# A gated linear recurrence followed by a gated feed-forward layer on one core: a new order of the first part, channel loads in two pieces of 48 rows, and two state copies on another engine

## The chip, the cores and the metric

The kernel runs on one core of a Trainium2 chip. Its engines work side by side, each through its own instructions in program order, and wait for one another by semaphores: TensorE (PE, with its weight loads PEld), VectorE (DVE), ScalarE (ACT), GpSimd (POOL), and SyncE (SP), which here only issues DMA transfers. The metric is the device time of one execution in microseconds (us), median of several runs. Lower is better.

## The reference

Cut to what matters: a recurrence over 768 steps for 4 batches and 8 heads of size 48, whose result goes through a feed-forward layer with a sigmoid gate.

```
for t in range(S):
    cur = einsum('bhd,bhe->bhde', u * k[t], v[t])
    y[t] = einsum('bhd,bhde->bhe', r[t], state + cur)
    state = w * state + einsum('bhd,bhe->bhde', k[t], v[t])
x = y.transpose(0, 2, 1, 3).reshape(3072, 384)
out = (sigmoid(x @ w_gate) * (x @ w_val)) @ w_out      # 384 -> 1536 -> 384
```

## The kernel before

The recurrence is done in 12 chunks of 64 steps. A chunk has two groups of heads (g = 1 first, then g = 0), so there are 24 groups n = 0 to 23; even n are g = 1. For a group, TensorE makes scores between the chunk's steps, applies them and the state to the values, and adds the chunk's own products to the state. The results of two chunks fill a tile of 512 columns, x, for the feed-forward layer, which runs over 12 blocks f of 128 hidden units. All 32-bit products there are split into a high and a low part, three matmuls for one. The weights come as 64-bit words and are turned into those two parts on the chip (once, in the first part of the program).

The first part (groups 0 to 7, all weights, and the feed-forward work of the first tile) is written out by hand: the text `START` is a list of steps, each a letter and a number, and every engine gets its instructions in the order of this list. After it, a loop carries the other five tiles. The steps that this document names:

- `L.n`, `X.n`, `W.f`: SP issues the load of a group's channels (`load_channels`, r and k with channels on partitions: 128 rows of 4 KB, of which rows 48 to 63 and 112 to 127 are padding), of its tokens (k and v with steps on partitions), of a block of weights.
- `A.n` (ACT), `R.n` (POOL) or `Rv.n` (DVE), `k.n` (DVE, in place): scale the channels; `T.n` (POOL) or `Tv.n` (DVE): scale the tokens.
- `Z.n` (PE): scores, 64 matmuls into the one tile `sc`; `K.n` (DVE): copy them through masks (L355). `I.n` (PE): from state and scores to y, two banks of PSUM; `O.n` (PE): the chunk's products, into the same two banks. `h.n` (ACT), `l.n` (DVE): high and low part of y into the tile x; `F.n`: six or fewer small transfers from SBUF to SBUF that move 16 rows of x to their places (fills). `d.n` (ACT) decays the state, `s.n` (DVE) adds the products to it, or for the first chunk (n = 0, 1) copies them, L428.
- `c.f` (ACT), `j.f` (DVE, three operations), `w.f` (ACT), `o.f` (POOL) or `ov.f` (DVE): unpack a block of weights; `c0`, `j0`, `w0`, `o0`, `o0v` do halves of block 0.
- `U.i` (PE, L495): the up products of work item i, two banks of PSUM; `g.i` (ACT), `m.i` (DVE), `H.i` (ACT), `q.i` (POOL) or `qv.i` (DVE): the gate and its two parts; `D.i` (PE, L533): the down products. Items 0 and 1 are blocks 0 and 1 for the first chunk's 256 columns, 2 and 3 the same for the second, and item i from 4 is block i - 2 for all 512.
- `tk`, `ti`, `tp` (DVE), `tt` (PE), `tn` (ACT): tables of powers of w. `tc` (POOL, ACT): constants.

Tiles come from pools: channels had three buffers in turn, tokens three, and the PSUM pool `ring`, which holds the banks of `I` and `U`, has three banks. A step that takes a bank waits until the last reader of what was in it is done.

Of the kernel before, what the change touches and what calls it, by code (L numbers as in the profile page):

```python
# [9 lines left out]
F32 = mybir.dt.float32  # L10
# [28 lines left out]


START = """
L.0 tc A.0 tk ti.1 tp W.0 X.0 k.0 Rv.0 c0.0 ti.0 c0.1 L.1 j0.1 A.1 Z.0 K.0 tt L.2 k.1 I.0 Rv.2 A.2
R.1 X.1 tn h.0 T.0 X.3 Z.1 k.2 T.1 l.0 L.3 K.1 O.0 s.0 j0.0 W.1 A.3 I.1 w0.1 o0v.1 h.1 l.1 L.4 R.3
w0.0 c.1 X.2 F.0 Z.2 K.2 W.2 o0.0 O.1 s.1 j.1 Tv.3 X.6 U.0 g.0 c.2 m.0 I.2 k.3 w.1 W.4 W.7 ov.1 d.2
T.2 O.2 h.2 l.2 X.4 s.2 H.0 Z.3 K.3 A.4 q.0 k.4 R.4 c.4 j.2 U.1 g.1 I.3 O.3 L.7 L.5 m.1 d.3 h.3 H.1
l.3 A.5 D.0 w.2 R.5 Z.4 T.4 s.3 K.4 F.2 U.2 k.5 g.2 m.2 q.1 D.1 H.2 U.3 g.3 Z.5 j.4 m.3 X.5 I.4 O.4
W.3 L.6 T.5 H.3 d.4 R.6 X.7 ov.2 h.4 q.3 q.2 c.3 K.5 W.5 s.4 w.4 l.4 U.4 j.3 D.2 g.4 m.4 A.6 H.4 D.3
ov.4 qv.4 w.3 I.5 O.5 d.5 W.6 h.5 c.5 D.4 k.6 ov.3 l.5 c.6 s.5 U.5 A.7 g.5 j.5 w.5 U.6 g.6 j.6 w.6
ov.5 c.7 Z.6 m.5 m.6 K.6 U.7 H.5 qv.5 W.9 g.7 j.7 H.6 D.5 qv.6 o.6 I.6 Tv.6 w.7 W.8 k.7 d.6 D.6 O.6
m.7 Rv.7 H.7 s.6 h.6 c.8 l.6 ov.7 U.8 g.8 q.7 F.6 j.8 c.9 j.9 D.7 w.8 U.9 g.9 ov.8 Z.7 W.11 m.9 w.9  # L50
U.10 H.9 m.8 W.10 H.8 qv.8 D.8 g.10 o.9 K.7 q.9 D.9 m.10 I.7 c.11 j.11 c.10 H.10 qv.10 D.10 h.7 T.7
d.7 j.10 w.10 O.7 l.7 s.7 U.11 w.11 ov.10 g.11 ov.11 U.12 m.11 H.11 F.7 g.12 m.12 q.11 H.12 q.12 D.11
U.13 g.13 D.12 m.13 H.13 q.13
"""


# [1 line left out]
def rwkv_then_moe(ctx: ExitStack, tc: tile.TileContext, wd, ch, tk, rt, ut, wt, rk0, vn0, wd0, out):  # L58
    nc = tc.nc
# [7 lines left out]
    ring = ctx.enter_context(tc.tile_pool(name="ring", bufs=3, space=PSUM))  # L67
    pacc = ctx.enter_context(tc.tile_pool(name="pacc", bufs=1, space=PSUM))
    main = ctx.enter_context(ExitStack())
    ach = main.enter_context(tc.tile_pool(name="ach", bufs=3))  # L70
    atk = main.enter_context(tc.tile_pool(name="atk", bufs=3))
    adk = main.enter_context(tc.tile_pool(name="adk", bufs=2))
    xp = main.enter_context(tc.tile_pool(name="xp", bufs=2))
# [332 lines left out]
    def states(n):  # L406
        g = GROUPS[n][1]
        st = state[0:112, 8 * g * D : 8 * (g + 1) * D]
        return g, st.rearrange("q (p s x) -> q p s x", p=2, s=2)
# [129 lines left out]
    def accumulators():  # L539
        return [pacc.tile([P, 512], F32, name=f"acc{d}") for d in range(3)]  # L540
# [77 lines left out]
    for step in START.split():  # L618
        name, _, arg = step.partition(".")
# [68 lines left out]
    with tc.If(bad != 0):  # L688
        with ExitStack() as g:
# [3 lines left out]
            st = gp.tile([P, NP, B, D], F32, name="st")  # L693
# [18 lines left out]
            with tc.For_i(0, NC) as c:  # L712
                for p in range(NP):
                    nc.sync.dma_start(
                        out=rkc[:, p].rearrange("q a b i -> q (a b i)"),
                        in_=rk0[bass.ds(c, 1), p].rearrange("o q x -> (o q) x"),
                    )
                with tc.For_i(0, C) as i:
                    for lo, side in ((0, 1), (64, 0)):
# [18 lines left out]
                    for lo in (0, 64):  # L738
                        y = one_bank()
# [11 lines left out]
                    out=xg[bass.ds(c, 1)].rearrange("o q p t -> (o q) p t"),  # L751
                    in_=yc.rearrange("q p b i -> q p (b i)"),
# [3 lines left out]
            with tc.For_i(0, NC, 2) as c:  # L756
                for j in range(3):
                    for to, lo, n, p in (
# [3 lines left out]
                            out=xr[to : to + n, j],  # L762
                            in_=xg[bass.ds(c, 2), lo : lo + n, p].rearrange("c q t -> q c t"),
# [4 lines left out]
                m = Moe(x, accumulators(), slice(0, 512))  # L768
# [103 lines left out]
```

## Time and profile before

| what | value |
|---|---|
| median of 3 runs | 541.75 us (540.87 to 541.93) |
| the profiled execution's own time | 540.73 us |
| its span in the trace | 538.9 us |
| busy in the span: PE / PEld / DVE | 518.4 / 425.6 / 216.4 us |
| busy in the span: ACT / POOL | 171.3 / 174.8 us |
| chain that ended last: PE, DMA, DVE | 91%, 4%, 1% of the span |
| HBM read, written | 40.12 MB, 4.72 MB |

The span is what the trace covers; the profiled execution's own time is 1.8 us longer, and the median of the runs shown is 1.0 us above that. A busy time of PE counts pipelined matmuls from start to modelled end, so PE can read as busy while it works below its pace. Times in the trace are counted from the start of the span.

### The profile page before, as it was taken

What the parts mean: (1) busy time and instruction counts of PE and PEld (TensorE: products, weight loads), DVE (VectorE), ACT (ScalarE), POOL (GpSimd) and SP (SyncE); (2) the same over time, 40 slices, a digit from 0 to 9 for tenths busy, and PEclk for the clock granted to TensorE, in tenths of its full rate; (3) what the DMA queues carried; (4) which work ended last, traced back from release to release, by engine and by line L of the source; (5) the groups of instructions that cost most, each with busy time, mean ns of one, the idle gap of its engine ahead of it and who ended that gap; (6) DMA issues with size and microseconds to landing.
All of it is one profiled execution on the core that took longest, in us unless ns stands there. A gap on an engine that the chain in (4) does not pass through costs nothing.

```text
span 538.9 us, 12058 instructions
## 1 busy us (share of the span) xinstructions
PE 518.4 (96%) x5268; PEld 425.6 (79%) x5268; DVE 216.4 (40%) x375; ACT 171.3 (32%) x354; POOL 174.8 (32%) x159
## 2 busy tenths in 40 slices
PE   2889999999999999999999999999999999999996
PEld 2778878788788887888888888888888887888885
DVE  7999989912343342432413414313414311111111
ACT  5485755522132322231332222312322212221121
POOL 3424022122814444244145144143242311111120
PEclk9999999999999999999999999999999999999998
DMA  8895705053022214220303402203400001100001
GB/s 318 312 338 217 286 1 186 15 205 128 2 86 86 66 50 144 85 74 12 95 3 103 145 5 82 65 30 106 144 1 16 11 2 19 60 1 1 0 1 63
DMA packets 15706, 48.03 MB, mean 89 GB/s; under 512 B 2368, under 2 KB 5056, under 8 KB 14240
## 3 DMA queue, kind: packets, MB, share of 16 engines
q1 hardware_dynamic: 15360, 46.81, 25.4%
q8 instruction: 43, 0.70, 0.5%
q10 hardware_dynamic: 288, 0.39, 0.2%
q14 instruction: 15, 0.12, 0.1%
HBM read 40.12 MB, written 4.72 MB: 83 GB/s over the span
## 4 chain that ended last, share of the span: by engine, by line
PE 91%; DMA 4%; DVE 1%; SPq 1%; issue 1%; ACT 0%; POOL 0%; DVEq 0%; ACTq 0%; POOLq 0%
PE ring L495 56%; PE acc L533 27%; PE ring L313 5%; PE sc L341 2%; DMA xt<-xt 1%; DMA chan<-in_ch 1%; PE sc L396 1%; DMA wr<-in_wt 1%; SPq L457 1%; PE sc L533 1%; POOL dec L294 0%; DVE wf L236 0%; DVE wx L246 0%; ACT wx L243 0%; ACT wf L229 0%
## 5 line engine op out<-in xcount | busy, mean ns | idle before, releaser
L495 PE MATMUL ring<-xt,wx 128*128 128x512 f32 (+1 forms) x1332 | 316.4, 391 | 1.4 <-DMA xt<-xt 1.2
L495 PEld LDWEIGHTS ring<-xt,wx 128*128 128x128 f32 x1332 | 246.1, 190 | 56.6 <-issue 1.3
L517 POOL TENSOR_TENSOR h<-sg,h 128x512 fp32r<-128x512 f32 (+1 forms) x68 | 86.7, 1276 | 298.8 <-ACT h L513 298.8
L533 PE MATMUL acc<-h,wx 128*128 128x512 f32 (+1 forms) x666 | 161.1, 383 | 0.0
L508 DVE TENSOR_TENSOR sg<-ring,sg 128x512 f32<-128x512 f32 (+1 forms) x74 | 49.9, 676 | 275.6 <-PE ring L495 275.6
L533 PEld LDWEIGHTS acc<-h,wx 128*128 128x128 f32 x666 | 119.6, 188 | 24.4
L504 ACT ACTIVATE sg<-ring 128x512 f32<-128x512 f32 (+1 forms) x74 | 43.4, 587 | 184.3 <-PE ring L495 181.2
L513 ACT CAST h<-sg 128x512 fp32r<-128x512 f32 (+1 forms) x74 | 45.3, 613 | 112.0 <-DVE sg L508 111.1
L415 ACT ACTIVATE state<-state,every 112x96 f32<-112x96 f32 x80 | 23.5, 365 | 26.2 <-PE ring L313 26.2
L294 POOL TENSOR_TENSOR dec<-chan,every 128x512 f32<-128x512 f32 x21 | 25.9, 1233 | 17.0 <-DMA chan<-in_ch 12.7
L453 DVE TENSOR_TENSOR xt<-ring,xt 112x256 fp32r<-112x256 f32 (+1 forms) x52 | 20.0, 419 | 24.9 <-ACT xt L449 24.4
L341 PE MATMUL sc<-dec,chan 48*64 48x64 f32 x768 | 17.4, 231 | 7.9 <-DVE dec L294 7.9
L355 DVE COPY_PREDICATED score<-masks,sc 128x512 f32<-128x512 int32 x32 | 23.9, 745 | 1.5 <-PE sc L341 0.6
L449 ACT CAST xt<-ring 112x256 fp32r<-112x256 f32 (+1 forms) x52 | 17.1, 373 | 19.6 <-PE ring L313 17.0
L341 PEld LDWEIGHTS sc<-dec,chan 48*64 48x64 f32 x768 | 15.0, 145 | 9.3 <-DVE dec L294 7.9
L313 PE MATMUL ring<-score,toks 64*48 64x64 f32 (+1 forms) x768 | 18.7, 230 | 3.7 <-POOL dec L294 1.6
L304 POOL TENSOR_TENSOR toks<-toks,tabn 128x384 f32<-128x384 f32 x20 | 21.1, 1059 | 1.7 <-ACT tabn L194 1.6
L313 PEld LDWEIGHTS ring<-score,toks 64*48 64x48 f32 (+1 forms) x768 | 15.3, 133 | 5.1 <-POOL dec L294 1.8
L313 PEld LDWEIGHTS ring<-dec,state 48*48 48x48 f32 (+1 forms) x704 | 12.4, 127 | 8.3 <-issue 7.4
L300 DVE TENSOR_TENSOR chan<-chan,every 128x512 f32<-128x512 f32 x24 | 17.2, 715 | 0.9 <-ACT dec L273 0.9
L246 POOL TENSOR_TENSOR wx<-wf,wx 128x1152 fp32r<-128x1152 f32 (+1 forms) x3 | 6.8, 2262 | 31.9 <-ACT wx L243 31.9
L282 POOL TENSOR_TENSOR dec<-dec,toks 128x384 f32<-128x384 f32 x16 | 16.3, 1017 | 1.2
(61 smaller groups left out, 260.0 us busy)
## 6 DMA issues: line engine op xcount, KB each, us to landing
wr<-in_wt SPq DMA_DIRECT2D x11, 1152.0 KB, 8.0
chan<-in_ch SPq DMA_DIRECT2D x24, 512.0 KB, 4.9
toks<-in_tk SPq DMA_DIRECT2D x24, 400.0 KB, 5.0
out_y<-wf SPq DMA_DIRECT2D x16, 256.0 KB, 2.3
dec<-in_rt SPq DMA_DIRECT2D x16, 192.0 KB, 2.6
xt<-xt SPq DMA_DIRECT2D x30, 64.0 KB, 2.3
wr<-in_wt SPq DMA_DIRECT2D x2, 576.0 KB, 5.4
xt<-xt SPq DMA_DIRECT2D x12, 32.0 KB, 5.1
```

Source lines behind the costliest of these rows:

```text
L294: eng.tensor_tensor(v4(t[:, 0]), v4(chan[n][:, 0]), bc2(table_of(n)), ALU.mult)
L304: eng.tensor_tensor(v4(k), v4(k), bc2(tabn[:, 4 * g : 4 * g + 4]), ALU.mult)
L313: nc.tensor.matmul(yb[n][bank][64 * half : 64 * half + m, cs], lhsT, rhs, start=first, stop=stop, skip_group_check=True,)
L341: nc.tensor.matmul(sc[64 * gm : 64 * gm + 64, be ^ gm, o : o + C], kk[row, cs : cs + C], rr[row, cs : cs + C], start=True, stop=True,)
L355: nc.vector.copy_predicated(t.rearrange("q (b m i) -> q b m i", b=2, m=4), masks[:, m].bitcast(I32).unsqueeze(1).unsqueeze(1).broadcast_to ...
L415: nc.scalar.activation(st[:, p, s], st[:, p, s], AF.Copy, scale=pw[0:112, 4 * g + 2 * p + s, 64:65],)
L495: nc.tensor.matmul(o[:, self.cols], w[a][:, g * DM + kt * P : g * DM + (kt + 1) * P], self.x[:, kt, b, self.cols], start=(k == 0), stop=(k ...
L504: nc.scalar.activation(sg[:, c], self.pair[f][0][:, c], AF.Sigmoid)
L508: nc.vector.tensor_tensor(sg[:, c], self.pair.pop(f)[1][:, c], sg[:, c], ALU.mult)
L513: nc.scalar.copy(out=h[:, 0, c], in_=sg[:, c])
L517: eng.tensor_tensor(h[:, 1, c], self.sg.pop(f)[:, c], h[:, 0, c], ALU.subtract)
L533: nc.tensor.matmul(acc[:, to], w[a][:, 2 * DM + d * P : 2 * DM + (d + 1) * P], h[:, b, cols], start=(f == 0 and k == 0 and self.cols.start ...
```

## The change

Three things are changed. First, `START` is a new list: the same work in another order, with one `o0`, one `T` and one `q` going from POOL to DVE (as `o0v`, `Tv`, `qv`) and one `ov` going from DVE to POOL (as `o`). Second, the channels have three named buffers that are passed on by hand (a buffer is free again after its group's scores); the first three loads are whole, and each later one is two transfers of 48 rows, which leave out the padding. Third, a step `sa` does the state copy of groups 0 and 1 with `nc.scalar.copy` (ACT) in place of `nc.vector.tensor_copy` (DVE).

```diff
-L.0 tc A.0 tk ti.1 tp W.0 X.0 k.0 Rv.0 c0.0 ti.0 c0.1 L.1 j0.1 A.1 Z.0 K.0 tt L.2 k.1 I.0 Rv.2 A.2
...
+tk ti.1 L.0 tc A.0 L.1 tp tt Rv.0 k.0 A.1 W.0 X.0 L.3 Z.0 c0.0 ti.0 k.1 R.1 K.0 I.0 c0.1 j0.0 j0.1
+X.1 Z.1 h.0 l.0 tn T.0 K.1 w0.0 L.2 A.2 O.0 o0v.0 X.2 W.1 w0.1 k.2 T.2 Rv.2 Tv.1 sa.0 I.1 o0v.1 A.3
+L.4 h.1 Z.2 l.1 O.1 c.1 k.3 j.1 Rv.3 F.0 W.2 sa.1 X.3 X.5 U.0 W.4 T.3 g.0 w.1 K.2 I.2 c.2 h.2 ov.1
...
-    ach = main.enter_context(tc.tile_pool(name="ach", bufs=3))
+    ach = main.enter_context(tc.tile_pool(name="ach", bufs=1))
...
+    CHANNELS = slice(0, D), slice(64, 64 + D)
     chan, toks = {}, {}
+    cbuf = [ach.tile([P, 2, 512], F32, name=f"chan{i}") for i in range(3)]
 
     def load_channels(n):
         c, g = GROUPS[n]
-        chan[n] = ach.tile([P, 2, 512], F32, name="chan")
-        nc.sync.dma_start(out=chan[n], in_=ch[c, g])
+        whole = len(chan) < 3
+        chan[n] = cbuf.pop(0)
+        for rows in (slice(0, P),) if whole else CHANNELS:
+            nc.sync.dma_start(out=chan[n][rows], in_=ch[c, g, rows])
...
+        cbuf.append(chan[n])
...
-    def add_state(n):
+    def add_state(n, copy=nc.vector.tensor_copy):
...
-                nc.vector.tensor_copy(st[:, :, s], y)
+                copy(out=st[:, :, s], in_=y)
```

Where instructions now stand. On DVE, at the start of the program (after the tables in `every`), the rows were the keys of group 0 (L300), its queries (L294), a reciprocal, half a block of weights (L235 to L237), and the first masked copy (L355):

```order
L156 TENSOR_TENSOR every<-every 128x8x32 x2
L300 TENSOR_TENSOR chan<-chan,every 128x512
L294 TENSOR_TENSOR dec<-chan,every 128x512
L172 RECIPROCAL every<-every 128x4x32
L235 TENSOR_SCALAR wf<-wf 128x576
L236 SCALAR_TENSOR_TENSOR wf<-wr,wf 128x576
L237 SCALAR_TENSOR_TENSOR wf<-wr,wf 128x576
L355 COPY_PREDICATED score_101<-masks,sc 128x512 x2
```

In the changed kernel (its lines are 4 or 5 higher) they are:

```order
L160 TENSOR_TENSOR every<-every 128x8x32 x2
L298 TENSOR_TENSOR dec<-chan_95,every 128x512
L304 TENSOR_TENSOR chan_95<-chan_95,every 128x512
L176 RECIPROCAL every<-every 128x4x32
L304 TENSOR_TENSOR chan_96<-chan_96,every 128x512
L360 COPY_PREDICATED score_104<-masks,sc 128x512 x2
L239 TENSOR_SCALAR wf<-wf 128x576
```

The queries now stand ahead of the keys, the keys of group 1 ahead of the first masked copy, and the weights behind it.

On PE, in the second half of the first part, the scores of group 7 (L341, `Z.7`) stood alone between two up products (L495, `U.9` and `U.10`):

```order
L495 MATMUL ring<-xt,wx 128x512 x18
L341 MATMUL sc<-dec,chan 64x64 x16
L341 MATMUL sc<-chan,dec 64x64 x16
L495 MATMUL ring<-xt,wx 128x512 x18
L533 MATMUL acc_428<-h,wx 128x512
```

Now they stand (L345) right behind the products of group 6 (L317, `O.6`), which themselves follow `I.6`, and ahead of a down product (L538, `D.6`):

```order
L317 MATMUL ring<-toks 64x48 x2
L317 MATMUL ring<-toks 48x48 x2
L345 MATMUL sc<-dec,chan_97 64x64 x16
L345 MATMUL sc<-chan_97,dec 64x64 x16
L538 MATMUL acc_427<-h,wx 128x512
```

Three separate groups of small matmuls, `I.6`, `O.6` and `Z.7`, have become one.

On SP, the rows ahead of the first fills (L457) were:

```order
L100 DMA chan<-in_ch 128x1024 x2
L105 DMA toks<-in_tk 128x800 x2
L100 DMA chan<-in_ch 128x1024
L223 DMA wr<-in_wt 128x1152
L100 DMA chan<-in_ch 128x1024
L105 DMA toks<-in_tk 128x800
L457 DMA xt<-xt 16x2x256 x6
```

And now:

```order
+L104 DMA chan_97<-in_ch 128x1024
+L109 DMA toks<-in_tk 128x800
+L104 DMA chan_95<-in_ch 48x1024 x2
+L109 DMA toks<-in_tk 128x800
+L227 DMA wr<-in_wt 128x1152
+L104 DMA chan_96<-in_ch 48x1024 x2
+L462 DMA xt<-xt 16x2x256 x6
```

One token load went behind the fills, and two channel loads ahead of them (`L.2` and `L.4`) are pairs of 48 rows.

## Rows read from the trace of the kernel before

**Rows 1.** Windows: busy us of each engine in stretches, with counts; granted clock; DMA.

```profile
core 0: us, PE busy (x) PEld busy (x) DVE busy (x) ACT busy (x) POOL busy (x), PEclk, DMA share, GB/s
20.00:40.00 20.00, 16.18 (x403) 14.62 (x403) 19.55 (x34) 13.24 (x32) 5.47 (x6) 1.00 0.88 315
40.00:60.00 20.00, 19.27 (x347) 17.08 (x346) 19.79 (x28) 12.74 (x28) 6.33 (x7) 1.00 0.72 269
60.00:80.00 20.00, 19.82 (x231) 15.61 (x231) 17.64 (x22) 11.54 (x19) 3.98 (x2) 1.00 0.18 74
104.00:160.00 56.00, 56.00 (x398) 45.31 (x391) 17.83 (x31) 15.14 (x27) 19.38 (x16) 1.00 0.32 104
```

**Rows 2.** Timeline of DVE, start: start us, duration, line, [idle before <-releaser].

```profile
6.54 0.69 DVE L300 TENSOR_TENSOR chan<-chan,every 128x512 f32<-128x512 f32 x1 [0.93 <-ACT dec L273]
7.15 0.68 DVE L294 TENSOR_TENSOR dec<-chan,every 128x512 f32<-128x512 f32 x1
7.76 0.94 DVE L172 RECIPROCAL every<-every 128x128 f32<-128x128 f32 x1
...
15.32 1.49 DVE L355 COPY_PREDICATED score<-masks,sc 128x512 f32<-128x512 int32 x2 [0.60 <-PE sc L341]
```

**Rows 3.** Timeline of DVE, 16 to 56 us.

```profile
16.71 0.60 DVE L428 COPY state<-ring 112x192 f32<-112x192 f32 x2
...
19.55 0.75 DVE L246 TENSOR_TENSOR wx<-wf,wx 128x576 fp32r<-128x576 f32 x1
...
27.37 0.55 DVE L304 TENSOR_TENSOR toks<-toks,tabn 128x384 f32<-128x384 f32 x1
...
36.96 0.42 DVE L508 TENSOR_TENSOR sg<-ring,sg 128x256 f32<-128x256 f32 x1
37.29 1.72 DVE L453 TENSOR_TENSOR xt<-ring,xt 48x256 fp32r<-48x256 f32 x4
...
41.02 1.25 DVE L300 TENSOR_TENSOR chan<-chan,every 128x512 f32<-128x512 f32 x1
...
50.66 0.75 DVE L235 TENSOR_SCALAR wf<-wf 128x1152 int32<-128x1152 int32 x1
...
54.12 0.68 DVE L508 TENSOR_TENSOR sg<-ring,sg 128x512 f32<-128x512 f32 x1
```

**Rows 4.** Timeline of PE matmuls, 7 to 42 us.

```profile
8.80 1.08 PE L341 MATMUL sc<-chan,dec 48*64 48x64 f32 x32
...
23.02 4.21 PE L495 MATMUL ring<-xt,wx 128*128 128x256 f32 x18
...
35.13 0.57 PE L313 MATMUL ring<-toks 64*64 64x48 f32 x29
...
39.24 2.53 PE L495 MATMUL ring<-xt,wx 128*128 128x256 f32 x18 [1.18 <-DMA xt<-xt]
```

**Rows 5.** Timeline of PE weight loads, 46 to 105 us: starts of groups of small matmuls.

```profile
46.95 0.17 PEld L313 LDWEIGHTS ring<-dec,state 48*64 48x64 f32 x5 [0.57 <-issue]
...
58.90 8.31 PEld L495 LDWEIGHTS ring<-xt,wx 128*128 128x128 f32 x36
67.58 0.56 PEld L341 LDWEIGHTS sc<-dec,chan 48*64 48x64 f32 x32 [0.37 <-issue]
...
78.84 0.55 PEld L313 LDWEIGHTS ring<-toks 64*64 64x64 f32 x32 [0.35 <-issue]
...
103.50 0.54 PEld L313 LDWEIGHTS ring<-toks 64*64 64x64 f32 x32 [0.35 <-issue]
104.09 0.99 PEld L495 LDWEIGHTS ring<-xt,wx 128*128 128x128 f32 x5
```

**Rows 6.** Timeline of ACT: the nearest copy from PSUM.

```profile
12.87 0.51 ACT L194 COPY tabn<-acc 128x192 f32<-128x192 f32 x2
```

**Rows 7.** DMA, 3 to 12 us (whole loads only): packets; q1's share of 16 engines.

```profile
DMA packets 1004, 3.55 MB, mean 395 GB/s; under 512 B 106, under 2 KB 106, under 8 KB 1004
q1 hardware_dynamic: 1004, 3.55, 98.5%
```

**Rows 8.** DMA, 105.1 to 107.5 us (fills of 16 rows only).

```profile
DMA packets 57, 0.13 MB, mean 55 GB/s; under 512 B 25, under 2 KB 25, under 8 KB 57
q1 hardware_dynamic: 57, 0.13, 34.0%
```

More of the change, by code (lines that the diff above doesn't have):

```diff
@@ L41 @@
 START = """
-L.0 tc A.0 tk ti.1 tp W.0 X.0 k.0 Rv.0 c0.0 ti.0 c0.1 L.1 j0.1 A.1 Z.0 K.0 tt L.2 k.1 I.0 Rv.2 A.2
[L43 to L53, printed above, removed]
+tk ti.1 L.0 tc A.0 L.1 tp tt Rv.0 k.0 A.1 W.0 X.0 L.3 Z.0 c0.0 ti.0 k.1 R.1 K.0 I.0 c0.1 j0.0 j0.1
+X.1 Z.1 h.0 l.0 tn T.0 K.1 w0.0 L.2 A.2 O.0 o0v.0 X.2 W.1 w0.1 k.2 T.2 Rv.2 Tv.1 sa.0 I.1 o0v.1 A.3
+L.4 h.1 Z.2 l.1 O.1 c.1 k.3 j.1 Rv.3 F.0 W.2 sa.1 X.3 X.5 U.0 W.4 T.3 g.0 w.1 K.2 I.2 c.2 h.2 ov.1
+m.0 Z.3 L.5 L.7 H.0 W.3 l.2 R.4 O.2 q.0 K.3 d.2 s.2 j.2 U.1 g.1 I.3 D.0 T.5 A.4 k.4 h.3 l.3 w.2 d.3
+Z.4 F.2 o.2 O.3 m.1 X.4 H.1 X.7 s.3 R.5 U.2 A.5 L.6 qv.1 W.11 g.2 m.2 U.3 c.3 D.1 K.4 H.2 qv.2 k.5
+c.4 D.2 Tv.4 g.3 I.4 m.3 d.4 O.4 j.3 H.3 s.4 h.4 l.4 Z.5 K.5 A.7 q.3 w.3 ov.3 U.4 g.4 m.4 D.3 I.5 O.5
+d.5 j.4 R.7 H.4 W.5 s.5 X.6 h.5 l.5 W.6 W.7 w.4 q.4 ov.4 c.5 U.5 W.10 g.5 m.5 A.6 Tv.6 R.6 H.5 c.6
+D.4 j.5 U.6 qv.5 D.5 W.8 W.9 k.6 w.5 g.6 k.7 Z.6 m.6 ov.5 c.7 H.6 j.6 U.7 g.7 K.6 I.6 O.6 q.6 d.6 h.6
+m.7 H.7 Z.7 w.6 j.7 qv.7 T.7 D.6 ov.6 w.7 s.6 D.7 K.7 c.8 l.6 U.8 o.7 g.8 j.8 U.9 w.8 m.8 g.9 ov.8
+m.9 H.8 q.8 U.10 c.9 D.8 H.9 q.9 j.9 g.10 c.10 m.10 j.10 w.9 F.6 I.7 d.7 O.7 H.10 w.10 qv.10 D.9 D.10
+ov.9 s.7 c.11 o.10 h.7 l.7 F.7 U.11 g.11 j.11 m.11 H.11 q.11 w.11 U.12 g.12 ov.11 m.12 H.12 D.11 U.13
+g.13 m.13 H.13 q.12 D.12 qv.13
 """
@@ L600, in rwkv_then_moe @@
         "k": keys, "T": token_keys, "Z": scores, "K": keep, "I": apply, "O": outer,
-        "d": decay_state, "s": add_state, "h": x_high, "l": x_low, "F": fills, "D": finish,
+        "d": decay_state, "s": add_state, "sa": lambda n: add_state(n, nc.scalar.copy), "h": x_high, "l": x_low, "F": fills, "D": finish,
         "tc": constants, "tk": channel_table, "ti": inverses, "tp": token_powers,
```

## The prediction

> **What bounds the kernel now.** I read the stretches first. From 104 us on PE is busy for the whole of each stretch, and the change leaves that part as it is [rows 1]. Ahead of it PE falls short: of 20 us it is busy 16.18 in 20 to 40 us, then 19.27 and 19.82. In 20 to 60 us it is DVE that never rests (19.55 and 19.79 of 20), and the DMA share is high in the same place (0.88, 0.72) [rows 1]. So the start is bound by DVE's chain, with loads close behind, and PE's own pace takes over at about 40 us. The seam is U.2, the first product of the second chunk: its input is the low part l.3, which DVE does from 37.29 for 1.72 us, so until 39.01 [rows 3], and U.2 starts at 39.24, the trace naming the fills as what it waited for [rows 4]. Behind U.2 the matmuls follow each other, but each group of small matmuls that comes after large ones starts with a bubble: 0.37 us at 67.58, 0.35 at 78.84, 0.35 at 103.50 [rows 5]. The end is therefore the time of U.2, plus PE's work behind it, plus the bubbles and waits in it. Both orders have the same matmuls ahead of U.2 and behind it: I.0 to I.3, Z.0 to Z.4, U.0, U.1, D.0 ahead.
>
> **Term 1, the start up to U.2.** DVE's chain runs without a break from 6.54 us to l.3, but for one wait of 0.60 us for Z.1 [rows 2]. What changes in it:
> - The queries of group 0 go ahead of the keys. DVE stood idle 0.93 us before the keys, waiting for ACT [rows 2]; the queries (0.61 us from their start at 7.15 to the next at 7.76) need the load alone and fit in. Gain 0.61.
> - The masked copy K.0 now comes soon after Z.0, which it must wait for. Z.0 needs keys and queries: it can start when the keys end, 6.54 + 0.69 = 7.23, against 7.83 before, so its second half, which ended at 8.80 + 1.08 = 9.88 [rows 4], ends near 9.3. DVE by then has done keys, reciprocal and the keys of group 1: 6.54 + 0.61 + 0.95 + 0.6 = 8.7. A new wait of 0.65; but K.1 no longer waits (two halves of weights stand ahead of it), so the old 0.60 goes. Net cost 0.05.
> - Work ahead of l.3: in come o0v.0 (0.75), Tv.1 (0.55) and the queries of group 3 (0.68); out go both state copies (0.60 each), Tv.3 (0.55) and m.1 (0.42) [rows 2, 3]. Net -0.2.
> - l.3 so ends at 39.01 - 0.61 + 0.05 - 0.2 = 38.25. But O.3, which shares its banks with l.3, now comes after it and ahead of U.2: 0.6 us on PE [rows 4]. U.2 starts at 38.9, not 39.24: **-0.3 us**. The bounds: down to 38.4 if durations are all at their shortest in the new order (the chain holds slower stretches where POOL is at work, 1.25 us for keys that else take 0.69 [rows 2, 3]); up to 39.6 if two more of them fall so.
>
> The state copies on ACT have no row; the nearest are two ACT copies of 128x192 from PSUM, 0.51 us together [rows 6], against 0.60 on DVE [rows 3], and ACT is busy only 13 of 20 us [rows 1]. I take 0.5. They free the banks for I.1 and for U.0's second half; sa.0 can run from O.0's end (near 16.5) and I.1 is ready near 16.9, so the cover is 0 to 0.4 us, and without it I.1 would start up to 0.5 later, hidden as long as l.1 waits for its turn on DVE (near 19.9).
>
> **Loads.** At the whole loads' pace, 9 us x 16 engines x 98.5% for 3.55 MB, a 4 KB row costs an engine 0.164 us [rows 7]. A whole load is 8 rows to an engine, 1.31 us; a pair of 48 rows is 6, so 0.98. The only rows with fewer partitions are the fills, 16 rows: 2.4 us x 16 x 34.0% for 57 - 25 = 32 packets of 4 KB, 0.41 us each [rows 8]. A pair could so cost 2.45. I take the low end, since the packets come from HBM as those of the whole loads do, and keep the other for the range. Ahead of the fills for U.0 this makes: one token load less (400 KB at 395 GB/s, 1.04 us) and two pairs at -0.33 each, so the fills come 1.7 us earlier; at the high end 1.2 later. U.0 itself is ready at about 22.8, when O.1 behind l.1 is done, against 23.02 before [rows 4], so the low end is hidden. The loads ahead of the fills for U.2 leave over 2 us in either case. A second transfer costs SP another issue, which nothing waits for.
>
> [...]
>
> **Term 2, behind U.2.** Groups of small matmuls behind large ones, from U.2 to U.11, before: [Z.5 I.4 O.4], [I.5 O.5], [Z.6], [I.6], [O.6], [Z.7], [I.7], [O.7], eight. After: [I.4 O.4 Z.5], [I.5 O.5], [Z.6], [I.6 O.6 Z.7], [I.7 O.7], five. Three bubbles of 0.35 to 0.37 less [rows 5]: **-1.07 us**. Besides, I.4 waited 0.57 us in its middle for a bank [rows 5]; two down products now stand ahead of it, so this may go too. I count it at nothing, as new waits of that size are likely, and keep it as a bound.
>
> Are there new waits? DVE's list behind U.2 has m.2 ahead of K.4 and m.4 ahead of j.4, so DVE stands idle until U.2 and U.4 end (about 1.7 and 1.0 us). The narrowest place behind is U.5: its second bank is free after l.5, and DVE does j.4 (54.12 - 50.66 = 3.46 [rows 3]), s.5 and half of l.5 between U.4's end and that, 0.25 + 0.62 + 3.46 + 0.53 + 0.4 = 5.3 us. PE meanwhile has D.3 (1.1), I.5 and O.5 with their bubble (2.4) and U.5's first half (a quarter of the 8.31 us of U.5 and U.6 [rows 5], 2.1): 5.6. It holds by 0.3 us. The same count gives 1.1 at U.7 and 0.6 at D.7.
>
> **The sum.** -0.3 - 1.07 = -1.4. The profiled execution took 540.73, so the same one would take 539.3; the median of the runs shown is 541.75, and I forecast **540.4 us**. Less than 0.2% (1.08 us) can't be told from no change here.
>
> **Rivals.**
> - **The new waits take it back.** Place: DVE behind U.2. It idles some 3 to 4 us there that it did not before, and if it comes 1 us late to U.5 or D.7, most of term 2 is gone: -1.4 + 0.3 to 1.1, near 541.3. For it: the margins of 0.3 and 0.6. Against it: at U.7 and U.8 over 1 us.
> - **The pairs are slow.** At 0.41 us a row the fills land 1.2 us later than before and U.0 with them; h.2 and l.2 follow U.0, so U.2 moves too, by about 1.3: 541.65, no change that shows. For it: rows 8. Against it: all else in rows 7 and 8 differs too. [...]
> - **Slower: DVE is late by 3 us.** Where POOL works beside it DVE's keys took 1.25 instead of 0.69 [rows 2, 3]. One block 0 half and one token scaling moved to DVE, but POOL now does o.2 just beside K.4 to m.3. From U.2 to U.7 DVE has 26.8 us of work and about 4 us of waits; if contention adds 3 us, l.5, ov.5 and qv.7 are late and PE waits 2.7 us in sum: 541.75 - 1.4 + 2.7 = 543.0. It costs more than it gains from 1.7 us on. Against it: POOL's share there is as before, and before's DVE rows have their contention in them.
>
> **Chances and range.** Forecast as it stands 0.50; new waits 0.26; slow pairs 0.12; late DVE 0.12. Faster by over 0.2% is the first case, and hardly any of the others; slower by over 0.2% is the last and a rest of the third: 0.50 faster, 0.36 same, 0.14 slower. The low end is the sum of the favourable bounds: U.2 at 38.4 (-0.85), term 2 (-1.07), I.4's wait (-0.57), so -2.5: 539.2. The high end leaves out half of the late DVE: 542.4. The forecast's own case holds 539.2 to 541.1.
>
> **What would show it.** U.2 near 38.9 and preceded by O.3, with no wait for fills; 0.68 us queries beginning near 5.6; five bubbles instead of eight between U.2 and U.11, and U.11 near 102.7 instead of 104.09 [rows 5]; channel pairs landing at about 1.0 us apart when the queue is full. I am wrong if a pair takes near 2 us, if U.5's second half or D.7 waits for DVE, or if U.2 is not earlier although l.3 is.

## The result, and the profile after

The changed kernel is slower: 545.28 us in the median of 6 runs (544.32 to 547.40) against 541.74 for the kernel before (540.87 to 541.99), a ratio of 1.0069 with the interval 1.0047 to 1.0090. The forecast was 540.4 and the range ended at 542.4. The execution that was profiled is the longest of the six (547.40 us, span 545.6), so what it lost is 2 us more than what a middling one loses.

The stretches, in the columns of [rows 1]:

```profile
20.00:40.00 20.00, 17.55 (x482) 15.83 (x479) 18.57 (x30) 13.59 (x33) 5.28 (x5) 1.00 0.88 272
40.00:60.00 20.00, 17.04 (x266) 15.81 (x257) 13.77 (x23) 10.37 (x26) 5.84 (x4) 0.83 0.79 260
60.00:80.00 20.00, 19.57 (x232) 15.61 (x232) 18.85 (x22) 11.96 (x21) 5.66 (x4) 1.00 0.58 243
104.00:160.00 56.00, 55.82 (x438) 45.22 (x430) 22.25 (x35) 17.17 (x32) 20.53 (x16) 1.00 0.32 88
```

Read against [rows 1], only 40 to 60 us stands out: PE is busy 17.04 us instead of 19.27, DVE 13.77 instead of 19.79, and the granted clock is 0.83 where it was 1.00. The DMA share from 20 to 40 us is the same 0.88, but it moves 272 GB/s instead of 315: the queue was as busy and moved less. From 104 to 160 us PE is busy 55.82 us instead of 56.00, so little is lost there. The very end of the program is another matter, and comes last in this section.

The timeline of PE matmuls, with the rows that answer to [rows 4] (U.0, then the last of O.3, then U.2 and U.3 together):

```profile
24.52 3.77 PE L500 MATMUL ring<-xt,wx 128*128 128x256 f32 x18
39.72 0.66 PE L317 MATMUL ring<-toks 64*64 64x48 f32 x30 [0.41 <-DVE xt L458]
43.16 6.73 PE L500 MATMUL ring<-xt,wx 128*128 128x256 f32 x36 [2.78 <-DMA xt<-xt]
```

U.2 starts at 43.16 instead of 39.24, and PE stood idle for 2.78 us waiting for a fill. DVE was ready long before. Its rows, which answer to [rows 2, 3], are the queries of group 0, the keys of group 1, l.3 (done at 39.66) and m.2, which waits for U.2:

```profile
5.57 0.68 DVE L298 TENSOR_TENSOR dec<-chan,every 128x512 f32<-128x512 f32 x1
...
7.96 1.72 DVE L304 TENSOR_TENSOR chan<-chan,every 128x512 f32<-128x512 f32 x1
...
37.92 1.74 DVE L458 TENSOR_TENSOR xt<-ring,xt 48x256 fp32r<-48x256 f32 x4
...
47.44 0.42 DVE L513 TENSOR_TENSOR sg<-ring,sg 128x256 f32<-128x256 f32 x1 [4.88 <-PE ring L500]
```

What held the fills shows in the DMA issues from 30 to 36 us (KB each, and us from issue to landing):

```profile
wr<-in_wt SPq DMA_DIRECT2D x1, 1152.0 KB, 10.2
chan<-in_ch SPq DMA_DIRECT2D x2, 192.0 KB, 7.0
xt<-xt SPq DMA_DIRECT2D x3, 32.0 KB, 9.5
```

The block of weights is W.3, issued at 32.36 and landed at 42.58; the fills for U.2 stand right behind it and landed from 42.80 to 43.87. W.3 itself stands behind the pairs of L.5 and L.7, and L.7 could only be issued at 31.53, when the scores of group 3 had freed its buffer (the first row is SP's issues of both pairs, the second the end of Z.3 on PE):

```profile
25.55 6.76 SPq L104 DMA_DIRECT2D chan<-in_ch  x4
...
30.80 0.65 PE L345 MATMUL sc<-chan,dec 48*64 48x64 f32 x32
```

The pace of the queue while it held hardly anything but the first pair (12 to 14 us) was half of what whole loads gave in [rows 7], at a full share:

```profile
DMA packets 136, 0.39 MB, mean 197 GB/s; under 512 B 28, under 2 KB 28, under 8 KB 136
q1 hardware_dynamic: 136, 0.39, 101.6%
```

One load of both pieces is 393 KB, 2.0 us at 197 GB/s; a whole one is 524 KB, 1.33 us at the 395 GB/s of [rows 7]. The windows around U.2:

```profile
40.00:42.00 2.00, 0.38 (x26) 0.25 (x16) 1.60 (x4) 2.00 (x8) 2.00 (x1) 0.82 0.87 220
42.00:44.00 2.00, 0.84 (x4) 0.88 (x5) 0.56 (x1) 0.13 (x1) 1.60 (x2) 0.50 0.32 73
44.00:46.00 2.00, 2.00 (x11) 2.00 (x11) 0.00 (x0) 0.49 (x2) 0.00 (x0) 0.50 1.04 318
46.00:48.00 2.00, 2.00 (x12) 2.00 (x11) 0.56 (x2) 1.15 (x2) 0.00 (x0) 0.50 1.00 250
48.00:50.00 2.00, 2.00 (x18) 2.00 (x18) 1.97 (x4) 1.76 (x3) 0.00 (x0) 0.98 0.99 401
```

PE did little from 40 to 43 us, and then ran at the lower clock (0.50 until 48 us) for most of the 36 products of U.2 and U.3, in 6.73 us. A wait on a transfer (2.78 us) has become a wait and a slow stretch behind it.

That is not all that was lost. U.11 starts 4.58 us later than before (108.67 against 104.09 [rows 5]), but the span is 6.7 us longer. Most of the rest stands behind the last computation. These are the last rows of DVE, of the kernel before and of the changed one:

```profile
533.99 0.42 DVE L563 COPY sg<-sc 128x256 f32<-128x256 f32 x1
...
538.98 0.42 DVE L568 COPY sg<-sc 128x256 f32<-128x256 f32 x1
```

From the end of that row to the end of the span, with only the last of the result to move out, it is 4.5 us before (span 538.9) and 6.2 us now (545.6): 1.7 us more.

### The profile page after: what moved, and what is told of

It reads as the page before. It is cut to its first block, busy times and chain, and to the rows that moved or that the text cites. A ratio compares the mean times of both kernels' runs of the same rounds, so it can differ in the third digit from the quotient of the medians.

```text
span 545.6 us, 12119 instructions
## 1 busy us (share of the span) xinstructions
PE 520.5 (95%) x5268; PEld 427.9 (78%) x5268; DVE 218.9 (40%) x373; ACT 171.6 (31%) x358; POOL 179.0 (33%) x157
## 4 chain that ended last, share of the span: by engine, by line
PE 81%; DVE 2%; issue 1%; POOL 1%; ACT 0%; POOLq 0%; DVEq 0%
PE ring L500 49%; PE acc L538 25%; PE ring L317 4%; PE sc L345 2%; PE sc L401 1%; PE sc L538 1%; DVE wf L241 0%; DVE score L360 0%; POOL h L522 0%; DVE wf L240 0%; DVE wx L250 0%; POOL dec L298 0%; POOL dec L286 0%; POOL dec L284 0%; DVE sg L513 0%
## 5 line engine op out<-in xcount | busy, mean ns | idle before, releaser
L522 POOL TENSOR_TENSOR h<-sg,h 128x512 fp32r<-128x512 f32 (+1 forms) x67 | 88.7, 1323 | 311.1 <-ACT h L518 300.7
L538 PE MATMUL acc<-h,wx 128*128 128x512 f32 (+1 forms) x666 | 160.7, 382 | 0.0
L538 PEld LDWEIGHTS acc<-h,wx 128*128 128x128 f32 x666 | 119.7, 188 | 24.4
L317 PE MATMUL ring<-score,toks 64*48 64x64 f32 (+1 forms) x768 | 18.9, 230 | 4.5 <-DVE score L360 3.4
L317 PEld LDWEIGHTS ring<-score,toks 64*48 64x48 f32 (+1 forms) x768 | 15.4, 133 | 5.8 <-issue 3.6
L241 DVE SCALAR_TENSOR_TENSOR wf<-wr,wf 128x1152 int32<-128x1152 int32 (+1 forms) x13 | 19.1, 1473 | 0.4
L345 PE MATMUL sc<-dec,chan 48*64 48x64 f32 x768 | 17.5, 231 | 0.3 <-POOL dec L298 0.2
L317 PEld LDWEIGHTS ring<-dec,state 48*48 48x48 f32 (+1 forms) x704 | 12.0, 127 | 7.2 <-issue 6.3
L233 ACT ACTIVATE wf<-wr 128x1152 f32<-128x1152 f32 (+1 forms) x13 | 15.4, 1186 | 4.3 <-issue 2.1
L284 POOL TENSOR_TENSOR dec<-dec,ub 128x384 f32<-128x384 f32 x16 | 16.7, 1041 | 0.0
```

The costliest lines, as they stand in the source:

```text
L317: nc.tensor.matmul(yb[n][bank][64 * half : 64 * half + m, cs], lhsT, rhs, start=first, stop=stop, skip_group_check=True,)
L345: nc.tensor.matmul(sc[64 * gm : 64 * gm + 64, be ^ gm, o : o + C], kk[row, cs : cs + C], rr[row, cs : cs + C], start=True, stop=True,)
L522: eng.tensor_tensor(h[:, 1, c], self.sg.pop(f)[:, c], h[:, 0, c], ALU.subtract)
L538: nc.tensor.matmul(acc[:, to], w[a][:, 2 * DM + d * P : 2 * DM + (d + 1) * P], h[:, b, cols], start=(f == 0 and k == 0 and self.cols.start ...
```

## The experiments

Theory 1: the pieces of 48 rows move at half pace, the fills land late, U.2 waits and the clock falls. Theory 2, the rival: the new order of the queue is at fault, which puts W.3 ahead of the fills for U.2 (W.4 stood there before too). Theory 3: the state copies on ScalarE. A fourth, that a second transfer costs something whatever its rows, came up with e5. Every kernel was timed against runs of the kernel before on the same chip (their medians lie between 541.74 and 542.50), and the ratio is to those runs, so two kernels are better compared by their ratios. U.2, the clock (mean granted in 40 to 60 us) and the end (us from the end of DVE's last row to the end of the span) are of its one profiled execution.

| kernel | us | ratio to before, interval | U.2 at | clock | end |
|---|---|---|---|---|---|
| before | 541.74 | 1 | 39.24 | 1.00 | 4.5 |
| after | 545.28 | 1.0069 (1.0047 to 1.0090) | 43.16 | 0.83 | 6.2 |
| e1 after, whole loads | 541.57 | 0.9997 (0.9982 to 1.0012) | 39.90 | 1.00 | 4.5 |
| e2 before, 48-row pairs | 545.17 | 1.0053 (1.0033 to 1.0072) | 40.67 | 0.91 | 6.3 |
| e3 after, W.3 behind the fills | 545.09 | 1.0054 (1.0031 to 1.0076) | 40.32 | 1.00 | 6.0 |
| e4 after, 64-row halves | 548.97 | 1.0134 (1.0111 to 1.0156) | 43.77 | 0.89 | 5.5 |
| e5 after, even and odd rows | 543.76 | 1.0035 (1.0020 to 1.0050) | 41.87 | 1.00 | 5.9 |
| e6 after, one piece of 112 rows | 542.37 | 1.0013 (0.9995 to 1.0030) | 42.14 | 1.00 | 4.6 |
| e7 before, one piece of 112 rows | 544.58 | 1.0054 (1.0029 to 1.0080) | 42.45 | 0.88 | 4.5 |
| e8 e1 with Rv.1 | 541.04 | 0.9991 (0.9976 to 1.0006) | 40.57 | 1.00 | 4.5 |
| e9 after, two pieces by columns | 543.18 | 1.0019 (1.0002 to 1.0037) | 41.00 | 0.91 | 6.7 |
| e10 e8 with W.3 behind the fills | 539.70 | 0.9964 (0.9944 to 0.9984) | 38.75 | 1.00 | 4.6 |
| e11 after, pairs from group 8 on | 542.63 | 1.0006 (0.9992 to 1.0021) | 40.58 | 0.91 | 6.0 |
| e12 e10, state copies on VectorE | 545.02 | 1.0057 (1.0040 to 1.0075) | 44.21 | 1.00 | 4.7 |
| e13 e1 with a 64-byte second transfer | 543.07 | 1.0025 (1.0010 to 1.0040) | 41.45 | 1.00 | 6.1 |
| e14 e10 with 48-row pairs | 544.71 | 1.0030 (1.0013 to 1.0048) | 40.29 | 1.00 | 6.2 |

The last column falls in two groups without overlap: 4.5 to 4.7 us in the seven kernels with one transfer for each load, 5.5 to 6.7 in the nine that use two, in the loop alone (e11) or in the first part too, and whatever the pieces. So a second transfer has a price in these kernels, and it is paid at the end of the program. Why the program ends later is not shown.

One profile of a kernel is not its median. e1 and e11 have the same first part, and their profiles differ by 0.68 us at U.2 and by 2.27 at U.11 (103.29 and 105.56). Differences of that size between two profiles show nothing by themselves.

**e1, whole loads in the new order.**

```diff
-        whole = len(chan) < 3
+        whole = True
```

> The changed kernel with every channel load whole again (128 rows), all else the same. Theory 1, the pairs are slow (the first pair landed in 0.99 + 0.97 us, a whole load in 1.30): the four pairs ahead of the fills for U.2 cost 4 x 0.65 = 2.6 us of the queue. Without them W.3 lands near 39 instead of 42.58, the fills for U.2 wait for l.3 alone, U.2 starts near 39 to 40 instead of 43.16, the granted clock in 44 to 50 us is 1.00 instead of 0.66, and the time is 540 to 541.5 us. Theory 2, the new order of the queue (W.4 and W.3 ahead of the fills for U.2) is what costs: U.2 stays at 42.5 or later and the time at 544 to 546. Theory 3, state copies on ScalarE: no change, 545.

The whole loss is gone, as theory 1 has it; the order with its ScalarE copies costs nothing without the pairs. Whole loads take away two things at once, though, the slow pieces and the second transfers (the end is 4.5 us again). The queue gave 375 GB/s where it had given 197 (12.6 to 13.6 us):

```profile
DMA packets 125, 0.37 MB, mean 375 GB/s; under 512 B 16, under 2 KB 16, under 8 KB 125
```

U.2 started at 39.90, later than the forecast 38.9, and the expected gain over the kernel before did not come. Two things show in the trace. The fills still landed behind W.3, at 39.60 to 40.50, while l.3 was done at 38.79. And the keys of group 1 took 1.72 us on DVE:

```profile
8.18 1.72 DVE L304 TENSOR_TENSOR chan<-chan,every 128x512 f32<-128x512 f32 x1
```

**e2, the pairs in the old order** (the kernel before with the changed kernel's three buffers and its `load_channels`).

```diff
+        whole = len(chan) < 3
+        chan[n] = cbuf.pop(0)
+        for rows in (slice(0, P),) if whole else CHANNELS:
+            nc.sync.dma_start(out=chan[n][rows], in_=ch[c, g, rows])
```

> The kernel before, its order and its state copies on VectorE, with the three named channel buffers and the pairs of 48 rows after the first three loads. Theory 1: four pairs ahead of the fills for U.2 (two of them ahead of those for U.0) cost 2.6 us there, U.2 starts at 41 to 42 instead of 39.24 and the time is 543.5 to 545. Theories 2 and 3 (the order, the state copies): U.2 stays near 39.2 and the time at 541.7.

As slow as the changed kernel: the pairs alone make the loss, in either order. Of the 4.8 us by which the span is longer than before (543.7), 1.8 stand at the end. U.2 is only 1.4 later in its profile, with waits of 1.78 and 0.31 for fills; the clock is 0.91 in 20 to 40 us and again in 40 to 60.

**e3, the queue's order.**

```diff
-m.0 Z.3 L.5 L.7 H.0 W.3 l.2 ...
-Z.4 F.2 o.2 ...
+m.0 Z.3 L.5 L.7 H.0 l.2 ...
+Z.4 F.2 W.3 o.2 ...
```

> The changed kernel, pairs kept, with the load W.3 moved on SP's queue from ahead of the fills for U.2 to right behind them. The fills then have the two pairs of L.5 and L.7 ahead of them, which landed at 38.97, and l.3, which ended at 39.66: U.2 should start near 40.7 instead of 43.16 by theory 1, and PE's idle time ahead of it be too short to cost clock: 541 to 543 us. By theory 2 (the queue's order alone) U.2 is back at 39 to 40 and the time at 540 to 541. If something else holds U.2 the time stays at 545.

U.2 came to 40.32 as expected and kept its clock, and the time did not follow (541.67 to 547.74 over its runs). The gain went into a new wait: the second half of U.5 stood 1.96 us for l.5, the place that the prediction called its narrowest. The rows are that half on PE, DVE's last operation of j.4, and GpSimd's queries beside it:

```profile
62.25 2.33 PE L500 MATMUL ring<-xt,wx 128*128 128x512 f32 x9 [1.96 <-DVE xt L458]
...
58.64 2.33 DVE L241 SCALAR_TENSOR_TENSOR wf<-wr,wf 128x1152 int32<-128x1152 int32 x1
...
59.73 2.29 POOL L298 TENSOR_TENSOR dec<-chan,every 128x512 f32<-128x512 f32 x1
```

That operation takes 1.36 us elsewhere (in e10, at 55.56). So neither theory's time came; that the fills held U.2 did. The price at the end stayed too (6.0 us).

**e4 and e5, what is slow in a piece.** Both move the rows of a whole load in two transfers of 64 rows.

```diff
-    CHANNELS = slice(0, D), slice(64, 64 + D)
+    CHANNELS = slice(0, 64), slice(64, P)            # e4
+    CHANNELS = slice(0, P, 2), slice(1, P, 2)        # e5
```

> The changed kernel with the pieces of each pair made 64 rows instead of 48, so that both together move the same rows as a whole load. If the rows of such a piece move at half pace (0.97 us for 48), a piece takes 1.3 us and a pair 2.6, four of them 2.6 us more ahead of U.2 than now: U.2 near 45 to 46 and the time 547 to 549. If a second transfer has a fixed price, and not a price for its rows, a pair stays at 1.95 us and the time at 545. If two pieces of 64 rows move as one whole load does (1.3 us), the time is that of the kernel with whole loads.

> The changed kernel with the two pieces of each load made the even rows and the odd rows (64 rows each, spread over all partitions) in place of the upper and the lower half. Bytes, rows and number of transfers are those of the 64-row pieces, which gave 549. Theory 1, a piece is slow because its rows lie in one half of the partitions: the 4 KB packets take 0.16 us instead of 0.32, a pair lands in 1.3 us like a whole load, and the time is that of whole loads, 541 to 542.5. Rival, a piece is slow because it is a piece (fewer rows in a transfer, or the price of a second transfer): packets at 0.32 us and 548 to 550 as with the 64-row halves.

They differ by 5.2 us, and only in which rows go together in a transfer: in which partitions it writes and, with them, in which places of HBM it reads. The pace while the first pair moved, e4 from 12 to 14.4 us:

```profile
DMA packets 169, 0.52 MB, mean 218 GB/s; under 512 B 31, under 2 KB 31, under 8 KB 169
q1 hardware_dynamic: 169, 0.52, 102.6%
```

and e5 from 12.3 to 13.2 us:

```profile
DMA packets 101, 0.31 MB, mean 347 GB/s; under 512 B 17, under 2 KB 17, under 8 KB 101
q1 hardware_dynamic: 101, 0.31, 103.5%
```

Both keep the queue at a full share (102.6 and 103.5%); in one half of the partitions they move 218 GB/s, over all of them 347. The pieces of 48 rows in the changed kernel, each in one half too, moved at 197. Whether the writing or the reading of such rows is slow, these two runs do not show. And e5 missed its number: at 543.76 it is still slower than whole loads, by 2.2 us. In its profile the end is 1.4 us longer than in e1, and the clock is 0.91 in 20 to 40 us, where the table does not show it (U.1, at 33.19, took 3.77 us; in e11, at a clock of 1.00, it took 2.41).

**e6 and e7, one transfer of rows 0 to 111.**

```diff
+    CHANNELS = (slice(0, 64 + D),)
```

> The changed kernel with each load after the first three as one transfer of rows 0 to 111 (it leaves out only the last 16 rows of padding). By theory 1 it is spread over nearly all partitions, 7 rows to an engine at 0.16 us, 1.15 to 1.25 us a load against 1.30 for a whole one: 0.1 us for each of the four loads ahead of U.2 less than with whole loads, so 541 to 542, the same as whole loads. If any number of rows under 128 is slow, 544 or more.

> The kernel before (order and state copies) with the three named buffers and the loads of 112 rows in one transfer. U.2 waited there for its fills, which landed 38.88 to 39.96, and l.3 ended at 39.01, so at most 0.2 us is to be had: 541.3 to 541.9, the same as before. If rows under 128 are slow in themselves, 543.5 or more, as with the pairs in that order.

One piece of 112 rows is no faster than 128. In e6 the queue gave 305 GB/s from 11.9 to 13.9 us:

```profile
DMA packets 187, 0.61 MB, mean 305 GB/s; under 512 B 25, under 2 KB 25, under 8 KB 187
q1 hardware_dynamic: 187, 0.61, 106.5%
```

A load that leaves out an eighth of the rows at four fifths of 375 GB/s takes longer than the whole one. In the new order the loss can't be told from nothing; in the old one (e7) it is 2.5 us, where 541.3 to 541.9 was expected: U.0 waited 0.42 us for its fills, U.1 1.97 for its weights, and the clock fell to 0.86 in 20 to 40 us.

**e8, the queries of group 1 on DVE** (whole loads).

```diff
-... ti.0 k.1 R.1 K.0 ...
+... ti.0 k.1 Rv.1 K.0 ...
```

> The changed order with whole loads, and the queries of group 1 done by VectorE behind its keys (Rv.1) in place of GpSimd beside them (R.1). With whole loads the keys of group 1 took 1.72 us on VectorE, at 8.18, while GpSimd did R.1 (8.17 for 1.18). If the two collide, keys take 0.69 and the queries 0.68 behind them, 0.35 less than now, and the chain up to l.3 and U.2 (39.9) is 0.3 us earlier: 541.2 if 541.6 is the time of whole loads. If they do not collide, VectorE's chain is 0.68 later and the time 542.2.

The durations are as expected: the keys take 0.69 us again where GpSimd does not do the queries beside them (in e1 it did, at 8.17 for 1.18 us, and they took 1.72), and keys and queries together end at 9.54 where the keys alone ended at 9.90.

```profile
8.24 0.69 DVE L304 TENSOR_TENSOR chan<-chan,every 128x512 f32<-128x512 f32 x1
8.85 0.69 DVE L298 TENSOR_TENSOR dec<-chan,every 128x512 f32<-128x512 f32 x1
```

Why the keys take longer beside GpSimd is not shown. The time moved by 0.5 us, which the intervals do not separate from e1, and U.2 (40.57) still waited 1.36 us for the fills.

**e10, that and W.3 behind the fills.**

```diff
+        whole = True
...
+... ti.0 k.1 Rv.1 K.0 ...
...
+m.0 Z.3 L.5 L.7 H.0 l.2 ...
+Z.4 F.2 W.3 o.2 ...
```

> The changed order with whole loads and Rv.1 (the best so far, 541.0, where U.2 at 40.57 still waited 1.36 us for its fills behind W.3, which landed at 39.97), and W.3 moved behind those fills. If the fills are all that holds U.2, it starts near 39.2 to 39.5 and the time is 539.8 to 540.3, faster than the kernel before. Rival: as in the run with pairs and W.3 behind the fills, VectorE then meets GpSimd's queries in another place (a join of weights took 2.33 us instead of 1.36 at 58.64), and the second half of U.5 waits 1 to 2 us for l.5: 541 to 542.

Faster than the kernel before by 0.36% (interval 0.16 to 0.56%), and the only kernel here that is. U.2 waits for no transfer, the clock stays at 1.00, and U.11 starts at 102.13 (the first row is of PE, the second of its weight loads):

```profile
38.75 4.53 PE L500 MATMUL ring<-xt,wx 128*128 128x256 f32 x36
...
102.13 8.34 PEld L500 LDWEIGHTS ring<-xt,wx 128*128 128x128 f32 x36
```

These are nearly the two numbers that the prediction gave for the changed kernel, 38.9 and 102.7.

**e11, pairs only in the loop.**

```diff
-        whole = len(chan) < 3
+        whole = n < 8
```

> The changed kernel with whole loads for groups 0 to 7 and pairs of 48 rows only from group 8 on, in the loop behind the first part. There the queue has gaps and PE sets the pace, so slow pairs should be hidden: 541 to 542, the same as with whole loads everywhere. If pairs cost time in the loop too, 543 or more.

The time can't be told from that of the kernel before, but lies above the 541 to 542 expected. In the loop the slow pairs are hidden: from U.11 (105.56) to the end of DVE's last row (536.00) it takes 430.4 us, and 430.5 with whole loads (e1, 103.29 to 533.76). The end is 6.0 us instead of 4.5. Its profile shows the clock once more. A wait of 0.98 us for fills ahead of U.2 was followed by a clock of 0.50 from 41 to 44 us and 6.11 us for the same 36 products that took 4.53 in e10, at 1.00:

```profile
40.58 6.11 PE L500 MATMUL ring<-xt,wx 128*128 128x256 f32 x36 [0.98 <-DMA xt<-xt]
```

**e12, the state copies back on VectorE** (e10 otherwise).

```diff
-... Rv.2 Tv.1 sa.0 I.1 o0v.1 A.3
-... F.0 W.2 sa.1 X.3 X.5 U.0 ...
+... Rv.2 Tv.1 s.0 I.1 o0v.1 A.3
+... F.0 W.2 s.1 X.3 X.5 U.0 ...
```

> The fastest version so far (changed order, whole loads, Rv.1, W.3 behind the fills for U.2: 539.7, U.2 at 38.75) with the state copies of groups 0 and 1 back on VectorE, in the places where the list has them now. If VectorE's chain sets U.2, the two copies of 0.60 put l.3 and U.2 1.2 later, near 39.9, and the time at 540.9. Rival: the chain has slack for one of them or both (VectorE may find its waits filled by them), U.2 stays within 0.3 of 38.75 and the time at 539.7 to 540; then the move of the copies to ScalarE is worth nothing by itself.

Both expectations missed: slower than e10 by 5.3 us, or 5.0 by the ratios. The copies were priced as DVE's work; what counts is where they stand in its program. On ACT they ran at 17.76 and 23.10 in e10. On DVE the first comes at 19.86, behind four other steps, and the second at 29.59, behind a block of weights, and PE waits for both:

```profile
20.26 1.01 PE L317 MATMUL ring<-score,toks 64*64 64x64 f32 x27 [2.10 <-DVE state L433]
...
30.00 2.29 PE L500 MATMUL ring<-xt,wx 128*128 128x256 f32 x9 [2.67 <-DVE state L433]
```

Other places on DVE were not tried, so this prices the move within this order, not ScalarE against VectorE.

**e9 and e13, what a second transfer costs.** e9 loads queries and keys apart, 128 rows of 2 KB each; e13 loads whole and adds a transfer that nobody reads.

```diff
-        for rows in (slice(0, P),) if whole else CHANNELS:
-            nc.sync.dma_start(out=chan[n][rows], in_=ch[c, g, rows])
+        for x in (slice(0, 2),) if whole else (slice(0, 1), slice(1, 2)):     # e9
+            nc.sync.dma_start(out=chan[n][:, x], in_=ch[c, g][:, x])
...
+        nc.sync.dma_start(out=chan[n], in_=ch[c, g])                          # e13
+        if not whole:
+            nc.sync.dma_start(out=extra[16 * (n % 2) : 16 * (n % 2) + 16, n // 2 : n // 2 + 1], in_=ch[c, g, 0:16, 0, 0:1])
```

> The changed kernel with each load after the first three in two pieces by columns: queries and keys apart, each 128 rows of 2 KB over all partitions in their plain order. It asks what the even and odd pieces still lost to whole loads (543.8 against 541.6), though their packets were as fast. If a second transfer has a price of its own on the queue (SP's issues, the transfers that it may have in flight), the time is 543 to 544.5 here too. If the price was that of the even and odd rows alone, it is 541.5 to 542.5, as with whole loads (rows of 2 KB may cost a little more than half of 4 KB). [...]

> The changed kernel with whole loads, and behind each load after the first three a second transfer of 64 bytes to a tile that nobody reads: the number of transfers is that of the pairs, the bytes are those of whole loads. If a second transfer has a price of its own (SP's issue, its place among the transfers in flight), the time is 543 to 544, as with pieces by columns (543.2) or by even and odd rows (543.8). If not, 541 to 542 as with whole loads, and the remainder of those two lies in how their rows move.

(The 64 bytes of e13 are 4 bytes in each of 16 partitions.) Both came out where a second transfer has a price of its own: 543.18 and 543.07, some 1.5 us above whole loads (1.2 and 1.5 by the ratios), with 64 bytes as with half a load. Their intervals overlap that of e1 a little, so the times alone do not settle it. The end of the program does. These are DVE's last rows in e1 and in e13, whose spans are 538.3 and 541.5:

```profile
533.34 0.42 DVE L568 COPY sg<-sc 128x256 f32<-128x256 f32 x1
...
534.95 0.42 DVE L570 COPY sg<-sc 128x256 f32<-128x256 f32 x1
```

The end takes 6.1 us in e13 and 6.7 in e9, against 4.5. That U.2 is 1.1 and 1.6 us later than in e1 shows less: part of it is the clock (in e13 the clock is 0.91 in 20 to 40 us and U.1 took 3.92 us; in e11, which has e1's first part, it is 1.00 and U.1 took 2.41), and 0.7 lies between e1 and e11.

**e14, the pairs in the best order** (e10 otherwise).

```diff
-        whole = True
+        whole = len(chan) < 3
```

> The fastest version (539.7: changed order, Rv.1, W.3 behind the fills for U.2) with the pairs of 48 rows in place of its whole loads. With whole loads its fills landed at 35.2 to 38.0 and U.2 started at 38.75 without a wait for them. Four pairs at 0.65 us more put them at 38 to 40.6: U.2 near 40 to 40.5 and the time 541 to 542, if the fills are all that the pairs delay. If the pairs delay the channels themselves too (ScalarE waited 0.94 us for the first pair in the changed kernel), 542.5 to 545.

The pairs cost 5.0 us by the medians and 3.6 by the ratios even where W.3 no longer stands ahead of the fills. U.2 at 40.29 is as expected, with no wait for a transfer; its profile (546.12, the longest of its 12 runs, which go down to 541.25) loses more as e3 did, 1.97 us at the second half of U.5, with the clock at 0.91 in 60 to 80 us, and 1.6 us at the end. How often the wait at U.5 happens was not measured.

## Why the prediction was wrong

- **The step that failed** is the one on loads: "The loads ahead of the fills for U.2 leave over 2 us in either case." A pair was taken at 0.98 us, the low end, and took about 2.0; but the sentence also gave the high end room, and there was none at either. Already in the kernel before the fills landed from 38.88 to 39.96, around and behind the end of l.3 at 39.01 [rows 3], and [rows 4] name them as what U.2 waited for. With whole loads in the new order (e1) they landed at 39.60 to 40.50, behind l.3 (38.79). The new list has as many blocks of weights and channel loads ahead of them as the old one, but W.3 now stands behind L.5 and L.7, which wait for buffers. With the pairs W.3 landed at 42.58 and the fills 3.2 to 3.4 us later than in e1. Of that 0.8 was there when L.7 was issued (31.53 against 30.70), 2.5 when it had landed (38.97 against 36.49), and the rest came while W.3 moved.
- **A term put at nothing** failed with it: "A second transfer costs SP another issue, which nothing waits for." The runs show some 1.5 us (e13 against e1), at the end of the program; in the profile of the changed kernel it is 1.7 us, about half of the 3.5 us between the medians. The prediction's path ended at PE's work and had nothing behind it.
- **The reason for the low end** was that "the packets come from HBM as those of the whole loads do". e4 against e5 shows that this was the wrong likeness: their packets come from HBM too, at 218 and 347 GB/s. What differs between them is which rows go together in a transfer. What happened was the rival of slow pairs, given 0.12, but priced at 541.65, no change that shows; its 0.41 us a row makes a pair 2.45 us [rows 8], and a pair took about 2.0.
- **What no rival had** is the end of the program and the clock. In the profiled run U.2 and U.3 took 6.73 us, with the clock at 0.50 until 48 us, instead of the 4.53 of e10 at 1.00, 2.2 more, on top of U.2's 3.9.
- **Term 1** (U.2 at 38.9) had its mechanism right and came true only in e10. In the changed kernel the queries fit ahead of the keys at 5.57 for 0.68, as said, but the keys of group 1 took 1.72 where 0.6 was counted, and l.3 ended at 39.66, not 38.25. With whole loads it ended at 38.79 (e1), and with Rv.1 as well at 38.10 (e10).
- **Term 2** held and was a little small: from U.2 to U.11 the kernel before took 64.85 us [rows 4, 5], e10 63.38, so 1.47 less against a forecast of 1.07 and a bound of 1.64. The changed kernel took 65.51 (43.16 to 108.67), 2.2 of it clock. In the kernel before six groups of small matmuls start with a bubble behind large ones, at 67.58, 75.11, 78.84, 90.08, 99.68 and 103.50, where the prediction counted eight; three fewer was right, and the changed kernel's weight loads show the three that are left, where five were counted:

```profile
75.38 0.56 PEld L345 LDWEIGHTS sc<-dec,chan 48*64 48x64 f32 x32 [0.35 <-issue]
...
80.85 0.54 PEld L317 LDWEIGHTS ring<-dec,state 48*64 48x64 f32 x32 [0.36 <-issue]
...
102.76 0.54 PEld L317 LDWEIGHTS ring<-dec,state 48*64 48x64 f32 x32 [0.35 <-DVE sg L513]
```

- **The state copies**: the duration was right (two in 0.54 us, 0.5 forecast), their worth was not. They were counted as 1.2 us of DVE work; in e10's order their place is worth 5.0 to 5.3 (e12).
- **The narrow places**: U.5's second half waited 0.26 us in e10 and about 2 in e3 and e14. The margin of 0.3 was judged rightly, and what eats it, DVE's slower operation beside GpSimd's queries (2.33 us in e3 and e14, 1.36 in e10), was named, but as another rival's.

## What to carry to other kernels

Count no load by its bytes alone: here 393 KB in two pieces took 2.0 us and a whole load of 524 KB 1.33. Look at which rows go together in a transfer (64 in one half of the partitions moved at 218 GB/s, 64 even or odd ones at 347), and do not price a form of transfer that the trace does not show by the source that it shares with others. Count the second transfer as well (some 1.5 us, e13 against e1), and read a trace to its last row: here a price was paid behind all computation (1.7 us in the changed kernel's profile). When an order is changed, list everything that stands ahead of the one transfer that the critical step waits for, and add it up from the landing times. Look at the clock behind a wait that stands ahead of a dense stretch: here a wait of 2.78 us was followed by 2.2 us more for the same products. And price a step moved to another engine by its place in that engine's program: two copies of 0.6 us on DVE cost 5.0 to 5.3 us (e12).

## What the runs showed of the hardware

- One transfer of 112 rows moved at 305 GB/s where whole loads of 128 gave 375, at a full share of the queue; I had expected the same pace for each row. Why is not shown.
- Two transfers of 64 rows in one half of the partitions each moved at 218 GB/s, two of 64 even and odd rows at 347.
- A second transfer with each load made the stretch behind the last computation 5.5 to 6.7 us long (nine kernels) instead of 4.5 to 4.7 (seven), even when it carried 64 bytes (e13: 6.1). The cause is open.
- The granted clock was 0.50 behind a wait of PE of 2.78 us (changed kernel, from 42 to 48 us) and behind one of 0.98 us (e11, from 41 to 44 us), and stayed at 1.00 behind one of 1.36 us (e8). What decides it is not shown.
